# Routing tables by one-hot products instead of scatters, and a reordered end, in a strided-attention and mixture-of-experts kernel

## The chip, the cores and the metric

The kernel runs on one core of one Trainium2 chip. A core has TensorE (PE, matrix products into PSUM), VectorE (DVE), ScalarE (ACT), GpSimd (POOL) and SyncE (SP), each with its own instruction queue that runs in order; engines wait for each other through semaphores. The metric is the device time of one execution in microseconds (us). Profiles come from one execution that the hardware profiler recorded.

## The reference, cut to what matters

```python
# q, k, v: (8 batches, 8 heads, 576 positions, 64); the first 4 heads use mask_local, the others mask_strided
rel = pos[:, None] - pos[None, :]
mask_local = (rel >= 0) & (rel < 32)
mask_strided = (rel >= 0) & (pos[None, :] % 32 == pos[:, None] % 32)
attn = softmax(where(mask, q @ k.T / 8, -1e9)); x = attn @ v          # x: (8, 576, 512)

logits = x @ w_gate                                # 8 experts
local_gate = sigmoid(x @ w_local)
for b, s in order:                                 # a token keeps its predecessor's expert or takes its own
    fresh_e = argmax(logits[b, s])
    e = fresh_e if s == 0 or local_gate[b, s] < 0.5 else prev_e
    prev_e = e
    out[b, s] = softmax(logits[b, s])[e] * (relu(x[b, s] @ w1[e]) @ w2[e])   # w1: 512x1024, w2: 1024x512
```

## The kernel before, in words

There are three stages: attention (to 199 us of the profile), the experts, and a slow path (`general`) behind a branch on `flag`, which these inputs don't take.

`attention` walks over 32 pairs of heads (8 batches, 4 pairs each; two local, two strided) in steps `n`. Step `n` computes `scores` of pair `n` (L252; for strided pairs a mask product L246 first), the exponential on ACT, for local pairs a mask product on DVE (L263), the transposes `turn_x` of pair `n - 2` (L317), and `values` of pair `n - 1` (L276) with its normalisation `norm` (L289, L290). At a batch's end come `logits` (L336) and one step later `gates` (L354 and a chain of small DVE operations), which leave probabilities and a code for each token. `store_x` writes x to the DRAM tensor `xd` from SP's queue. A dictionary `also` puts further work at the end of given steps; weight sums of the first expert (L703) run from step 9, two a step. Constants (the masks among them) are made before the loop. All this is emitted under a manual schedule: the order in the code is the order in each queue.

The router works in two rounds of four batches. `Router.steps` finds each token's expert with scans over the codes and gives the token a slot: an index `idx` made of expert, place and tile. In both rounds a slot table `T` in DRAM is then filled by `scatters`, 20 indirect DMAs from POOL's queue (L577), each writing 8 bytes (token number, gate) for up to 128 tokens. `fetch` (L643) reads the table back to SBUF after round 1, `table` (L647) clamps its token numbers, and the experts gather rows of `xd` by it. Because round 0 alone fills a known part of expert 0's and 1's first tiles, `early` computes just those four columns of 128 slots in SBUF instead: a one-hot matrix `lane(i)` (128 tokens by 128 places, L620), a matrix `put` (token values times a one-hot of the column, L615), and 20 accumulated matmuls (L627), whose five outputs are put together to token number and gate (L632 to L637).

`Experts.run` goes through the experts, each with tiles of 128 tokens. Two tiles make a pair, computed with Strassen's seven products: `pair_hidden` (L807 with DVE additions L795 and ACT's relu L794, L814) and `pair_output` (L843; k operations L854 to L857; scatter of output rows L763). While a pair's output runs, the next pair's rows, gathered by L737, are scaled (L743), transposed (L750, copied out in L751) and summed (L759). `steps` is a list of places inside the pair at which other work is emitted: weight sums of the next expert (L703), and in the first two pairs round 1 of the router. After two pairs a `tc.Switch` on a number read into registers by `choose` picks one of seven arms, for up to three further tiles: a pair, a `single` (L898, L909) or a `half` (L919, L935). Before, the first two pairs of the run are expert 0's and 1's early tiles, then come expert 1's and 0's second pairs with their switches, then for each expert 2 to 7 its first pair, and its second pair with the switch. `flag` is loaded and tested after the last arm.

Of the kernel before, what the change touches and what calls it, by code (L numbers as in the profile page):

```python
# [18 lines left out]
P = 128  # L19
B, H, S, DH = 8, 8, 576, 64  # L20
D = H * DH
# [73 lines left out]
def attention_then_scomoe(ctx: ExitStack, tc: tile.TileContext, qkl, qks, vl, vs, wg, q, k, vl2, vs2, wg2, w1, w2, out):  # L95
# [7 lines left out]
    with ExitStack() as fast:  # L103
        once = fast.enter_context(tc.tile_pool(name="once", bufs=1))
        router = Router(once, dram, tc, ident)
        one = Weights(once)
        spot = (once.tile([P, 2, D], F32, name="x0"), once.tile([P, 2, DK, P], F32, name="xt"),
                once.tile([P, 4, 2, P], F32, name="tt"))
        with tc.manual_schedule():
            moe = Experts(nc, tc, xd, w1, w2, out, ident, router, one, spot)  # L110
            with ExitStack() as part:
                attention(part, tc, qkl, qks, vl, vs, wg, xd, ident, router, moe)
            with ExitStack() as part:
                moe.run(part)
        flag = router.flag


    redo = nc.values_load(flag, min_val=0, max_val=P + N,
                          skip_runtime_bounds_check_because="a count of at most 128 rows and of pairs")
    with tc.If(redo > 0):  # L120
# [22 lines left out]
def attention(ctx, tc, qkl, qks, vl, vs, wg, xd, ident, router, moe):  # L143
# [49 lines left out]
    for n, c in ((GK, GC), (GL, GR)):  # L193
# [20 lines left out]
        else:  # L214
            nc.vector.tensor_copy(maskS[:, 2 * GK:], cls)

    fold = consts.tile([P, E + 1], F32, name="fold")
    nc.vector.tensor_reduce(fold, ident.rearrange("p (k x) -> p x k", k=DK)[:, 0:E + 1], axis=AX.X, op=Alu.add)


    ci = consts.tile([P, E], I32, name="ci")
    nc.gpsimd.iota(ci, pattern=[[-1, E]], base=E, channel_multiplier=0)
    down = consts.tile([P, E], F32, name="down")
    nc.vector.tensor_copy(down, ci)
    pi = consts.tile([P, CH], I32, name="pi")
    nc.gpsimd.iota(pi, pattern=[[E * P, CH]], base=E, channel_multiplier=E)
    pos8 = consts.tile([P, CH], F32, name="pos8")
    nc.vector.tensor_copy(pos8, pi)
    start = consts.tile([P, CH], F32, name="start")
    nc.vector.tensor_scalar(start, pos8, float(E), None, Alu.is_equal)  # L230
# [165 lines left out]
    also = {n: [] for n in range(len(units) + 3)}  # L396
    also[2] = [router.constants]
# [6 lines left out]
    also[n] += [lambda: early.extend(router.early(bank, moe.spot)), lambda: early.pop(0)()]  # L404
    for n in range(m + 1, m + 6):
        also[n].append(lambda: early.pop(0)())
    for i, do in enumerate(router.scatters(0)):
        also[m + i // 2].append(do)
# [5 lines left out]
    for n in range(len(units) + 3):  # L414
# [20 lines left out]
        for do in steps[:2] if n >= 9 else []:  # L435
# [12 lines left out]
class Router:  # L448


    def __init__(self, pool, dram, tc, ident):
# [6 lines left out]
        self.tok = f("tok", [P, CH, B, 2], I32)  # L458
# [9 lines left out]
        self.io, self.jc = f("io", [P, P], BF16), f("jc", [P, 2, EARLY])  # L468
        self.vals = f("vals", [P, CH, RB, 5], BF16)
        self.put = f("put", [P, CH * RB, 5, 2 * EARLY], BF16)  # L470
        self.pool = pool
        self.T = dram.tile([P * NT, 2], I32, name="slots")

    def constants(self):
# [19 lines left out]
        ids = pool.tile([P, CH, B], I32, name="ids")  # L494
        nc.gpsimd.iota(ids, pattern=[[P, CH], [S, B]], base=0, channel_multiplier=1)
        nc.vector.tensor_copy(self.tok[:, :, :, 0], ids)
        for name, pattern, mult, o in (("io", [[1, P]], 0, self.io), ("jc", [[E, 2], [1, EARLY]], 0, self.jc),
# [5 lines left out]
        nc.gpsimd.iota(self.tab[:, :, 0], pattern=[[0, NT]], base=SKIP, channel_multiplier=0)  # L503
        nc.gpsimd.iota(self.tab[:, :, 1], pattern=[[0, NT]], base=0, channel_multiplier=0)
        nc.gpsimd.dma_start(out=self.rows(0, XT, E), in_=self.tab.rearrange("p (k e) v -> p k e v", e=E))

    def rows(self, k0, k1, e):

        return self.T.rearrange("(k p e) v -> p k e v", p=P, e=E)[:, k0:k1, 0:e]

    def steps(self, r, bank):
# [39 lines left out]
        def back():  # L551
# [16 lines left out]
            nc.vector.tensor_copy(self.tok.bitcast(F32)[:, :, bs, 1], p)  # L568
# [3 lines left out]
    def scatters(self, r):  # L572
        def one(t, b):
            m = min(P, S - t * P)

            def do():
                s = self.nc.gpsimd.indirect_dma_start(  # L577
                    out=self.T, out_offset=bass.IndirectOffsetOnAxis(ap=self.idx[0:m, t, b:b + 1], axis=0),
                    in_=self.tok[0:m, t, r * RB + b], in_offset=None, bounds_check=P * NT - 1, oob_is_err=False)
                self.tc.declare_no_dep(s.ins, group="slots", reason="scatters write different slots")  # L580
                self.tc.add_to_no_dep_group("slots", s.ins)
            return do
        return [one(t, b) for b in range(RB) for t in range(CH)]

    def early(self, bank, spot):
# [4 lines left out]
        lo, hi, code, lof = f("elo", [P, n], I32), f("ehi", [P, n], I32), f("ecode", [P, n]), f("elof", [P, n])  # L590
        at, rest, got = f("at", [P, n, 2 * EARLY], BF16), f("rest", [P, CH, RB]), f("got", [P, 5, 2 * EARLY])
        num, skip, gs = f("num", [P, 2 * EARLY]), f("skip", [P, 2 * EARLY]), f("gs", [P, 2 * EARLY])
        idx, val = flat(self.idx), self.vals.rearrange("p t b v -> p (t b) v")

        room = (spot[1].rearrange("p a k x -> p (a k x)").bitcast(BF16), spot[2].rearrange("p i a x -> p (i a x)").bitcast(BF16))
        lane = lambda i: room[2 * i // n][:, i % (n // 2) * P:(i % (n // 2) + 1) * P]

        def where():
# [6 lines left out]
            nc.vector.tensor_tensor(at, across(self.jc.rearrange("p k e -> p (k e)"), [P, n, 2 * EARLY]),  # L605
                                    spread(code, [P, n, 2 * EARLY]), op=Alu.is_equal)

        def what():
            v = [self.vals[:, :, :, i] for i in range(5)]
            nc.vector.tensor_copy(v[2], self.p)  # L610
# [3 lines left out]
            for i in range(5):  # L614
                nc.vector.tensor_tensor(self.put[:, :, i], at, spread(val[:, :, i], [P, n, 2 * EARLY]), op=Alu.mult)  # L615

        def lanes(a, b):
            def do():
                for i in range(a, b):
                    nc.vector.tensor_scalar(lane(i), self.io, lof[:, i:i + 1], None, Alu.is_equal)  # L620
            return do

        def products():
            o = bank()[:, 0:10 * EARLY].rearrange("p (v j) -> p v j", v=5)
            for i in range(n):
                m = min(P, S - i // RB * P)
                nc.tensor.matmul(o, lhsT=lane(i)[0:m], rhs=self.put[0:m, i], start=(i == 0), stop=(i == n - 1))  # L627
            nc.vector.tensor_copy(got, o)

        def numbers():  # L630
            tab = self.tab1.rearrange("p k e v -> p (k e) v")
            nc.vector.scalar_tensor_tensor(num, got[:, 0], 64.0, got[:, 1], Alu.mult, Alu.add)  # L632
            nc.vector.tensor_tensor(gs, got[:, 2], got[:, 3], op=Alu.add)
            nc.vector.tensor_scalar(skip, num, 0.0, SKIP + 64.0, Alu.is_equal, Alu.mult)
# [869 lines left out]
```

## Time and profile before

| | |
|---|---|
| median of 3 runs | 739.37 us (734.49 to 740.71) |
| profiled execution | 738.92 us |
| its span, first to last instruction | 737.2 us |
| mean granted TensorE clock | 0.959 |
| TensorE busy | 683.0 us (93%) |
| VectorE, ScalarE, GpSimd busy | 353.4, 195.5, 134.7 us |
| attention, experts | 0 to 199.6 us, 199.6 to 737.2 us |

A line of the groups names source line, engine, operation, output and input tiles and a count; after the bar stand busy us and the mean ns of one, then the idle time before them and what ended it. In the chain of work that ended last each line is a start, a length and what ran. A line in order of time has start, length, engine, line and operation; brackets at its end give the engine's idle time before it and what it waited for ("issue": nothing that the profile shows). PEld is TensorE's weight load, which overlaps its products.

### The profile page before, as it was taken

The page shows a single profiled execution, that of the slowest core. Times are in us where ns is not written, and L with a number is a line of the kernel's source. Part 1 is how long each engine was busy: PE and PEld are TensorE (multiplying, and loading weights), DVE is VectorE, ACT ScalarE, POOL GpSimd, SP SyncE. Part 2 cuts the span into 40 slices and gives each one's busy share as a digit, 9 for nine tenths or more (in the row PEclk, how much of TensorE's full clock was granted, in tenths as well). Part 3 has the DMA queues.
Part 4 walks back from the last instruction along what each step waited for, and adds up shares of the span by engine and source line. Part 5 has one row for each costly group of instructions (what it writes and reads, how often), then busy time and mean ns, then how long its engine had stood idle before and what let it go on. Part 6 is the DMA issues. An engine that isn't in the chain of part 4 may idle for free.

```text
span 737.2 us, 14832 instructions
## 1 busy us (share of the span) xinstructions
PE 683.0 (93%) x6034; PEld 586.5 (80%) x6034; DVE 353.4 (48%) x843; ACT 195.5 (27%) x357; POOL 134.7 (18%) x150
## 2 busy tenths in 40 slices
PE   7999999497899699999999999999999999999992
PEld 5878887385698589985998899999589899789961
DVE  6568766272466534451463265455126646524300
ACT  2544443141321122212222123122322222222210
POOL 3000001405127330221121120221012012111010
PEclk9999999597699899999999999999999999999997
DMA  9797887731360022615321711720171262010010
GB/s 325 275 328 267 279 286 256 249 84 52 95 228 30 3 86 67 238 38 173 109 74 47 254 47 50 251 73 21 39 257 59 76 210 66 32 37 30 18 50 13
DMA packets 37803, 95.33 MB, mean 129 GB/s; under 512 B 5230, under 2 KB 14446, under 8 KB 37632
## 3 DMA queue, kind: packets, MB, share of 16 engines
q1 hardware_dynamic: 29616, 73.77, 29.0%
q0 software_dynamic: 7488, 19.56, 8.4%
q8 instruction: 66, 1.08, 0.6%
q14 instruction: 105, 0.86, 0.4%
q10 hardware_dynamic: 528, 0.07, 0.1%
HBM read 74.41 MB, written 19.49 MB: 127 GB/s over the span
## 4 chain that ended last, share of the span: by engine, by line
PE 79%; issue 7%; DVE 5%; DMA 3%; another core or an unknown queue 3%; ACT 1%; POOL 1%; SPq 0%; DVEq 0%; POOLq 0%; ACTq 0%
PE mps L843 26%; PE lps L807 25%; PE vps L276 5%; PE sps L252 4%; PE tps L317 3%; PE lps L898 3%; PE mps L909 3%; PE xps L750 2%; DMA w1t<-in_w_dram 2%; PE mps L935 2%; PE lps L919 1%; PE sps L246 1%; PE tps L336 1%; PE vps L354 1%
## 5 line engine op out<-in xcount | busy, mean ns | idle before, releaser
L763 POOL DMA_INDIRECT out_dram<-y,tab x40 | 45.5, 1138 | 323.9 <-DVE y L795 217.4
L807 PE MATMUL lps<-tt,ws 128*128 128x128 f32 x768 | 91.5, 275 | 0.4 <-issue 0.2
L807 PEld LDWEIGHTS lps<-tt,ws 128*128 128x128 f32 x768 | 88.5, 192 | 0.8 <-DVE u L795 0.4
L843 PE MATMUL mps<-wt,k 128*128 128x256 f32 x384 | 85.6, 379 | 0.0
L843 PEld LDWEIGHTS mps<-wt,k 128*128 128x128 f32 x384 | 72.9, 190 | 9.9
L577 POOL DMA_INDIRECT slots<-tok,idx x40 | 40.9, 1023 | 147.5 <-DVE tok L568 135.9
L807 PE MATMUL lps<-xt,w1t 128*128 128x128 f32 x512 | 64.8, 281 | 2.6 <-ACT y L941 1.4
L807 PEld LDWEIGHTS lps<-xt,w1t 128*128 128x128 f32 x512 | 62.1, 196 | 6.1 <-ACT y L941 2.8
L795 DVE TENSOR_TENSOR h<-lps,u 128x512 f32<-128x512 f32 x48 | 33.2, 691 | 66.5 <-PE lps L807 57.3
L843 PE MATMUL mps<-w2t,h 128*128 128x256 f32 x256 | 61.3, 383 | 0.0
L737 POOL DMA_INDIRECT x<-xd,gi x40 | 40.4, 1009 | 112.5 <-PE lps L807 34.9
L252 PE MATMUL sps<-qk 64*128 64x96 f32 (+2 forms) x704 | 55.4, 288 | 4.9 <-issue 4.1
L252 PEld LDWEIGHTS sps<-qk 64*128 64x128 f32 (+2 forms) x704 | 45.5, 188 | 14.8 <-issue 12.5
L256 ACT ACTIVATE e<-sps 128x576 f32<-128x576 f32 (+1 forms) x64 | 41.2, 651 | 58.4 <-PE sps L252 40.8
L843 PEld LDWEIGHTS mps<-w2t,h 128*128 128x128 f32 x256 | 48.1, 193 | 6.0
L794 ACT ACTIVATE h<-h 128x512 f32<-128x512 f32 x48 | 30.3, 630 | 75.5 <-DVE h L795 71.7
L794 ACT ACTIVATE h<-lps 128x512 f32<-128x512 f32 x28 | 16.5, 594 | 86.8 <-PE lps L807 58.8
L795 DVE TENSOR_TENSOR u<-lps,p 128x512 f32<-128x512 f32 x16 | 11.1, 692 | 57.9 <-PE lps L807 32.3
L807 PE MATMUL lps<-xt,ws 128*128 128x128 f32 x256 | 33.1, 285 | 6.0 <-DVE h L795 6.0
L743 ACT ACTIVATE x<-x,tab 128x512 f32<-128x512 f32 (+1 forms) x40 | 27.2, 718 | 40.6 <-DMA x<-xd,gi 26.9
L807 PEld LDWEIGHTS lps<-xt,ws 128*128 128x128 f32 x256 | 31.5, 201 | 6.2 <-DVE h L795 6.2
L276 PE MATMUL vps<-vl,e 128*64 128x65 f32 x768 | 29.4, 235 | 7.0 <-issue 4.7
(222 smaller groups left out, 977.4 us busy)
## 6 DMA issues: line engine op xcount, KB each, us to landing
w1t<-in_w_dram SPq DMA_DIRECT2D x8, 2048.0 KB
w2t<-in_w_dram SPq DMA_DIRECT2D x8, 2048.0 KB
qk<-in_qkl_dram SPq DMA_DIRECT2D x16, 592.0 KB
qk<-in_qks_dram SPq DMA_DIRECT2D x16, 576.0 KB
vl<-in_vf_dram SPq DMA_DIRECT2D x8, 780.0 KB
vs<-in_vg_dram SPq DMA_DIRECT2D x8, 639.8 KB
xd<-xl SPq DMA_DIRECT2D x16, 288.0 KB
xd<-xs SPq DMA_DIRECT2D x64, 63.0 KB
```

Source lines behind the costliest of these rows:

```text
L252: nc.tensor.matmul(ps[0:m, h, c:c + w], lhsT=t[r, S + j * width:S + j * width + m], rhs=t[r, j * width:j * width + w], start=(u.local and ...
L256: nc.scalar.activation(e[0:kb, :, 0:n], ps[0:kb, :, 0:n], Act.Exp, bias=0.0, scale=1.0 / DH ** 0.5)
L276: nc.tensor.matmul(ps[a * HALF:(a + 1) * HALF, h, i], lhsT=u.e[0:m, h, q0:q0 + HALF], rhs=vt[0:m, j, 2 * i2 + h], start=(i == 0 and h == 0 ...
L317: nc.tensor.transpose(ps[:, t], src[:, t], ident)
L577: s = self.nc.gpsimd.indirect_dma_start(out=self.T, out_offset=bass.IndirectOffsetOnAxis(ap=self.idx[0:m, t, b:b + 1], axis=0), in_=self.t ...
L737: self.nc.gpsimd.indirect_dma_start(out=r.x[0:r.m, i], out_offset=None, in_=self.xd[0:r.rows], in_offset=bass.IndirectOffsetOnAxis(ap=r.gi ...
L743: self.nc.scalar.activation(r.x[0:r.m, i], r.x[0:r.m, i], Act.Copy, scale=r.gate[i][0:r.m])
L763: s = self.nc.gpsimd.indirect_dma_start(out=self.out, out_offset=bass.IndirectOffsetOnAxis(ap=r.si[i][0:r.m], axis=0), in_=y[0:r.m, i], in ...
L794: relu = lambda o, i: nc.scalar.activation(o, i, Act.Relu)
L795: add = lambda o, i, p: nc.vector.tensor_tensor(o, p, i, op=Alu.add)
L807: nc.tensor.matmul(ps[:, f], lhsT=m[:, kk, f * P:(f + 1) * P], rhs=v[:, kk], start=(start and f == 0 and kk == 0), stop=(kk == 1), skip_gr ...
L843: nc.tensor.matmul(ps[:, 0:256], lhsT=m[:, f], rhs=v[:, f], start=(start and f == 0), stop=(f == 3), skip_group_check=True)
```

## The change

1. The scatters, the DRAM table, its initial store, `fetch` and the old `table` go. A new `Router.table(r, ...)` builds all 56 columns of slots by one-hot products in both rounds. The second round adds onto the first's result. The column products (`put`) are now made on POOL, in 15 instructions a round; the lanes are made on DVE four at a time. Free tiles serve as room: the weight-sum tiles `t` of the weights at hand, `xt` or an output tile.
2. Masks: the second class mask (`classes(GL, GR)`) and other constants are made in steps 0 and 1 instead of before the loop.
3. The first expert's weight sums run from step 13, and the last eight of them (of w2) from step 29, after the table's products have read their room.
4. For experts 1, 0 and 7 the choice is loaded at the first place inside the pair rather than ahead of it.
5. The last expert runs its first pair with the switch and its second pair after the switch; `flag` is loaded inside that last pair, and the branch is told that the untaken side falls through.

```diff
-    redo = nc.values_load(flag, min_val=0, max_val=P + N, ...)
-    with tc.If(redo > 0):
+    with tc.If(redo > 0, preferred_fallthrough_block=False):
...
-    for n, c in ((GK, GC), (GL, GR)):
+    def classes(n, c):
...
+    classes(GK, GC)
...
+    also[0] = [lambda: classes(GL, GR)]
+    also[1] = [more_constants]
...
-    also[n] += [lambda: early.extend(router.early(bank, moe.spot)), lambda: early.pop(0)()]
+    lanes = moe.spot[1].rearrange("p a k x -> p (a k x)")
+    also[n] += [lambda: early.extend(router.table(0, bank, moe.W[0], lanes)), lambda: early.pop(0)()]
...
-    for i, do in enumerate(router.scatters(0)):
-        also[m + i // 2].append(do)
...
-        for do in steps[:2] if n >= 9 else []:
+        for do in steps[:2] if n >= (13 if len(steps) > 8 else m + 5) else []:
...
+    def table(self, r, bank, w, big):
...
         def where():
...
+            nc.vector.tensor_tensor(at, across(self.jc, [P, n, NT]), spread(code, [P, n, NT]), op=Alu.is_equal)
 
         def what():
...
+            for a in range(0, n, per):
+                m = min(n, a + per) - a
+                o = room[a // per][:, 0:m * wide].rearrange("p (i v j) -> p i v j", v=5, j=NT)
+                for i in range(5):
+                    nc.gpsimd.tensor_tensor(o[:, :, i], at[:, a:a + m], spread(val[:, a:a + m, i], [P, m, NT]), op=Alu.mult)
+
+        def some(a, b):
             def do():
+                for c in range(a, b, 4):
+                    l0, _, t = lanes[c >= nb]
+                    nc.vector.tensor_tensor(t[:, c - l0:c - l0 + 4], across(self.io, [P, 4, P]),
+                                            spread(lof[:, c:c + 4], [P, 4, P]), op=Alu.is_equal)
             return do
 
         def products():
+            o = bank()[:, 0:wide]
             for i in range(n):
                 m = min(P, S - i // RB * P)
+                nc.tensor.matmul(o, lhsT=lane(i)[0:m], rhs=put(i)[0:m], start=(i == 0), stop=(i == n - 1))
+            o = o.rearrange("p (v j) -> p v j", v=5)
+            if r:
+                nc.vector.tensor_tensor(got, o, got, op=Alu.add)
+            else:
+                nc.vector.tensor_copy(got, o)
...
+        return [where, what, some(0, n // 2 // 4 * 4), some(n // 2 // 4 * 4, n), products, numbers]
...
+            if index is None:
+                steps = [[lambda: chosen.append(choose(e))]] + steps
...
+        places[3] += [lambda: todo.extend(router.table(1, bank, W[1], other_y)), lambda: todo.pop(0)()]
+        for place in places[4:7]:
+            place.append(lambda: todo.pop(0)())
         output(self.first, W[0], pair_hidden(self.first, W[0], places), other, places)
         second = rows(0, 1, (2, 3))
-        places = slots(sums, [2, 2, 2, 2])
+        places = [[lambda: todo.pop(0)()]] + slots(sums, [3, 3, 2])
+        places[2] += [lambda: todo.pop(0)(), lambda: self.gather(second)]
...
-        places += [[lambda: next(arms), router.table, lambda: self.gather(second)]]
+        places += [[lambda: next(arms)]]
         h = pair_hidden(other, W[1], places)
-        router.fetch()
...
+        second = rows(0, e + 1, (2, 3))
+        rest(e + 1, W[e % 2], 1, nxt, [], second)
+        check = lambda: chosen.append(nc.values_load(router.flag, ...))
+        output(second, W[e % 2], pair_hidden(second, W[e % 2], [[check]]), None, [])
+        return chosen.pop()
```

## The prediction

> **What bounds the kernel now.** I read the page's totals and slices, then the chain that ended last, then stretches and the instructions in order of time where that chain leaves TensorE.
>
> ```profile
> PE 683.0 (93%) x6034; PEld 586.5 (80%) x6034; DVE 353.4 (48%) x843; ACT 195.5 (27%) x357; POOL 134.7 (18%) x150
> ...
> PEclk9999999597699899999999999999999999999997
> ...
> L577 POOL DMA_INDIRECT slots<-tok,idx x40 | 40.9, 1023 | 147.5 <-DVE tok L568 135.9
> ```
>
> TensorE (PE) is the bound, but the clock row dips in slices 7 to 13 (129 to 258 us): there PE isn't kept fed. The 40 scatters into the slot table all lie there. The chain says how much:
>
> ```profile
> 76.27 1.25 PE vps L354 x12
> 95.02 1.25 PE vps L354 x12
> 114.69 1.25 PE vps L354 x12
> 152.44 1.25 PE vps L354 x12
> 173.35 1.24 PE vps L354 x11
> 198.32 1.28 PE vps L354 x12
> ...
> 229.50 3.73 PE lps L807 x32
> ...
> 268.88 12.50 PE lps L807 x112
> ...
> 410.54 12.51 PE lps L807 x112
> ...
> 436.01 12.50 PE lps L807 x112
> ```
>
> L354 (gates) comes once a batch: 18.75 us apart undisturbed, then 37.75, 20.91 and 24.97. A pair of experts' tiles takes 436.01 - 410.54 = 25.47 us undisturbed, the second pair of the run 268.88 - 229.50 = 39.38. Inside the bad stretches (columns: stretch; us; busy and count of PE, PEld, DVE, ACT, POOL; clock; DMA share; GB/s):
>
> ```profile
> 176.00:181.00 5.00, 3.11 (x14) 2.21 (x15) 0.00 (x0) 0.00 (x0) 3.81 (x4) 0.50 0.03 4
> 240.00:245.00 5.00, 2.27 (x14) 1.56 (x12) 0.16 (x1) 0.60 (x1) 3.78 (x5) 1.00 0.02 1
> ```
>
> PE, DVE and ACT all stand while POOL issues scatters and the DMA engines are empty (3% and 2%). No data wait explains that: the releasers read "issue" or an unknown queue.
>
> [...] The trace agrees in kind: between 128 and 136 us it holds no instruction transfer at all, and the engines resume about when one lands. I read the stalls as fetches held up by the scatters' tiny writes; this is an inference. [...] The trace agrees only for POOL's side: a scatter issue of 0.97 us takes 1.41 when DVE runs such an operation.
>
> ```profile
> 218.69 0.69 DVE L855 TENSOR_TENSOR k<-k,h 128x512 f32<-128x512 f32 x1
> 218.83 1.41 POOL L577 DMA_INDIRECT slots<-tok,idx  x1 [0.30 <-issue]
> ...
> 222.34 0.91 POOL L577 DMA_INDIRECT slots<-tok,idx  x1 [0.30 <-issue]
> ```
>
> **The change part by part.** The sum is made against the profiled execution's 738.92 us (span 737.2 and 1.7 around it), 0.45 below the median of 739.37.
>
> *Scatters, table fetch and clamp go.* Batch 114.69 to 152.44: 37.75, less 18.75 and less 1.55 for the slot and back products that lie in it: 17.4 lost. Next batch: 20.91 less 19.4 (0.6 of old products in it): 1.5. The last batch has only the drain: by adding its PE pieces and the serial copies between them I estimate 14, so 24.97 - 14 = 11.0. Second pair: 39.38 - 25.47 = 13.9, which also holds the wait for table fetch and late gather (L737 at 260.75, its x scaled at 264 and 266). Sum 43.8. The 0.98 us table fetch and the initial table store leave POOL's queue without further gain.
>
> *Wide products come.* Per round 20 matmuls of 280 bf16 columns instead of 20 of 20 (0.60 us for all 20, round 0 only). [...] at L246's pitch, 252 columns in 0.18 us here, 4.0. I take 2.4: +4.2 in all, upper end +7.4. They are in PE's queue, so nothing hides them.
>
> *POOL builds the operands.* 15 multiplies a round, ten of 392 elements and five of 336: [...] PE waits for them in the products; every later PE instruction is queued behind that wait, and DVE's and ACT's work behind those. Round 0: the casts before them end near 132.5 on an unstalled clock; the products stand three steps on, near 145.4, so the cover is 12.9 us. Round 1: they start about 24 us after the first pair's start (16.8 to its output part, then DVE's six table operations 2.2, h and k operations 3.5, sums 1.3, casts 0.9, the first of them a little before that mark), and the products come at 33.4: cover 9.4. [...] in round 0 DVE has five 512-element comparisons (0.69 each, the price of such a DVE row) and six small operations of the gates in that window, [...] In round 1 fifteen such operations lie in it (six L703 sums of 0.68, five comparisons, four L759 of 0.42: 9.2): [...] I take the lock: 17.0, lower end 3.0.
>
> *DVE's own load.* The twenty 0.17 us comparisons and 0.84 of old products in round 0 become five of 0.69 and one 1120-element comparison of 1.3: much the same. In the second pair eight W[1] sums (5.5 us) now fall into three steps with numbers and arms, so k2 is 0.7 late; with a cooler clock after the waits I take +2.0 (0 to 4).
>
> *First masks first.* PE waits 2.29 us at 12.37 for e.
>
> ```profile
> 12.37 2.87 PE L276 MATMUL vps<-vl,e 128*64 128x65 f32 x48 [2.29 <-DVE e L263]
> ...
> 726.16 0.91 POOL L763 DMA_INDIRECT out_dram<-y,tab  x1 [8.59 <-ACT y L941]
> ```
>
> The moved work (twelve DVE operations of 0.20 to 0.29 and three on POOL, then seven more) doesn't vanish; norm of the first unit, at 14.24, moves only to about 14.3. So the next turn (17.42) gains about 1.3 of 2.3 (0 to 2.3).
>
> *Sums of W[0] moved.* The eight w1 sums from step 9 to 13 drop the 0.96 us wait for w1t; the eight w2 sums (0.68 each) go to steps 29 to 32, beside PE's drain. Taken as 0 (-1 to +1); if DVE is late there it shows in the last L354.
>
> *Choices inside a layer, second gather two places earlier.* Neither 268.88 nor 294 shows PE waiting at a choice, since matmuls queued before it keep PE busy: 0. Without that cover it is a gap as ACT's behind a switch at 537.69 (4.65 us), of which PE lost 0.35. The gather (two POOL issues of about 1 us) goes ahead of a scatter that nothing waits for: 0; its gain is in the 13.9.
>
> *Last pair behind the last switch, early flag.* Work is the same. After the last scatter's issue ends at 727.07 the span runs 10.1 us on. A row gather lands in about 2.05 us here (issued by 704.55, scaled at 706.62). Flag load and the taken branch leave the end; the landing stays, and an unconditional jump over the slow path too. I take -4.5, and -0.5 for one addition (0.42) in place of two copies (0.76): -5.0 (-2 to -7.5).
>
> Sum: -43.8 + 4.2 + 17.0 + 2.0 - 1.3 - 5.0 = -26.9, so 738.9 - 26.9 = 712.
>
> **The rivals.** *No lock.* POOL's reads go beside DVE's: waits 3.0 instead of 17.0, cooling and DVE 1.0 instead of 2.0: 738.9 - 41.9 = 697. For it: in this trace DVE was never held by POOL. Against: POOL here never reads wide operands beside DVE.
>
> *Multiplies dearer, or fetches still held.* At 1.3 us a multiply with the lock, about 12 us more wait; or gathers (40 stay) hold fetches as scatters did, and a quarter of the 43.8 stays: 11. Either gives about 724. For it: the stall at 171.4 began with two gathers. Against: pairs of gathers elsewhere show none.
>
> *POOL becomes the bound: slower.* Place: the wait at the two products. Without lock it is 30p - 22.3 us for a multiply of p us; all else gains 43.8 - 4.2 - 2.0 + 6.3 = 43.9, so it decides from p = 2.2. At p = 2.8: 738.9 - 43.9 + 61.7 = 757. For it: broadcast and bf16 operands on POOL aren't priced by any row. [...]
>
> **How the numbers follow.** Forecast 712: 0.52; no lock 697: 0.30; 724: 0.14; slower 757: 0.04. The range 694 to 723 takes in the first two with their bounds (products +3, tail and start about 3 either way) and leaves out half of the 724 case, the slower case and a little of the fastest. About 1% is what a measurement of this kernel can tell from no change (the three times shown spread over 0.8%). Faster by over 1% are the first three cases almost whole, 0.94; the fourth gives slower 0.04; 0.02 lies between.
>
> **What would show it.** Gates' L354 about 19 us apart from batch 4 to 6; PE's waits for POOL at the wide products, about 5 and 12 us; [...] second pair near 41 us (25.5, 12, 2.4 and 1); last scatter to end about 5.5 us. The prediction is wrong if stalls of all engines persist without scatters, if multiplies cost 2 us, or if POOL and DVE don't hold each other.

## The result and the profile after

In the first runs the median fell from 738.69 us (4 runs, 734.49 to 740.71) to 727.58 us (4 runs, 725.24 to 729.15). The ratio is 0.9864, with a 95% interval from 0.9824 to 0.9904: 11 us faster, where 27 were forecast. The profiled execution took 728.88 us (span 727.1). In the four groups of experiments below, each on a different chip, the kernel before takes 702 to 704 us (90 executions, 698 to 710). Run again beside it on one of these chips, the changed kernel is 20 us slower. That is the main finding.

The page of the changed kernel, with its totals, the clock row and the group of the new POOL multiplies:

```profile
PE 681.1 (94%) x6054; PEld 584.7 (80%) x6054; DVE 371.4 (51%) x842; ACT 195.2 (27%) x357; POOL 122.0 (17%) x135
...
PEclk9999999996999999999999999999999999999996
...
L606 POOL TENSOR_TENSOR wt<-wt,vals 128x392 bf16<-128x392 bf16 (+1 forms) x30 | 30.1, 1034 | 150.0 <-DVE wt L592 114.5
```

Between slices 7 and 13 one slice of the clock row is under 9 (slice 9, at 6), where the kernel before had four. The multiplies took 1.03 us on average. TensorE in order of time, from the gates of the fifth batch to the first pair:

```profile
113.67 1.25 PE L354 MATMUL vps<-fold,lT 128*128 128x9 f32 x12 [0.64 <-DVE sums L289]
...
135.86 1.25 PE L354 MATMUL vps<-fold,lT 128*128 128x9 f32 x12 [0.28 <-DVE sums L289]
...
144.58 0.41 PE L317 MATMUL tps<-ident,xs 128*128 128x128 f32 x2 [1.66 <-DVE sums L289]
...
146.98 2.08 PE L620 MATMUL tps<-wt,xt 128*128 128x280 bf16 x16
149.00 0.53 PE L620 MATMUL tps<-wt,wt 64*128 64x280 bf16 x3
...
161.02 1.25 PE L354 MATMUL vps<-fold,lT 128*128 128x9 f32 x12 [2.07 <-DVE sums L289]
...
178.58 2.19 PE L354 MATMUL vps<-fold,lT 128*128 128x9 f32 x12 [0.81 <-DVE lT L344]
180.70 1.65 PE L802 MATMUL lps<-xt,w1t 128*128 128x128 f32 x6
```

The gates are now 22.2, 25.2 and 17.6 us apart (37.8, 20.9, 25.0 before), and the first pair starts 18.8 us earlier. In round 0 PE waits for DVE, not for POOL itself. In the second pair the longest wait is for DVE too:

```profile
221.16 3.30 PE L802 MATMUL lps<-tt,ws 128*128 128x128 f32 x16 [4.19 <-DVE tt L754]
224.25 2.51 PE L620 MATMUL xps<-wt,y 128*128 128x280 bf16 x16
226.69 0.65 PE L620 MATMUL xps<-wt,wt 64*128 64x280 bf16 x4
...
241.90 3.51 PE L838 MATMUL mps<-w2t,h 128*128 128x256 f32 x8 [1.97 <-ACT q L854]
```

That POOL's multiplies hold DVE up (the prediction's "lock") is seen by laying two kernels side by side. First the changed kernel, in order of time, then the kernel with the multiplies on DVE (an experiment below), which has none on POOL:

```profile
204.37 16.45 POOL L606 TENSOR_TENSOR wt<-wt,vals 128x392 bf16<-128x392 bf16 x15 [33.31 <-issue]
...
206.43 2.23 DVE L698 TENSOR_TENSOR ws<-ws,w1t 128x512 f32<-128x512 f32 x2
...
208.58 2.59 DVE L612 TENSOR_TENSOR y<-io,elof 128x512 bf16<-128x512 bf16 x2
```

```profile
212.64 1.28 DVE L698 TENSOR_TENSOR ws<-ws,w1t 128x512 f32<-128x512 f32 x2
213.84 1.28 DVE L612 TENSOR_TENSOR y<-io,elof 128x512 bf16<-128x512 bf16 x2
```

The same two DVE operations take 2.2 to 2.6 us instead of 1.28 while POOL multiplies. Set against operations of the same form elsewhere in the changed kernel's trace, the 29 DVE operations that overlap POOL's multiplies in round 0 took 4.5 us longer in sum, and the 20 in round 1 took 7.4 us longer. The trace puts no wait of any engine down to a multiply itself: they cost PE time by way of DVE.

The last lines in order of time show the end of the work:

```profile
710.47 0.42 DVE L790 TENSOR_TENSOR y<-mps,v 128x256 f32<-128x256 f32 x1 [0.97 <-PE mps L838]
711.67 0.98 POOL L758 DMA_INDIRECT out_dram<-y,tab  x1 [0.90 <-POOLq L117]
```

The last scatter's issue ends at 712.65 and the span at 727.1: 14.4 us, against 10.1 before. The forecast was 5.5.

### The profile page after: what moved, and what is told of

It is laid out like the page before. It is cut to its first block, busy times and chain, and to the rows that moved or that the text cites. A ratio compares the mean times of both kernels' runs of the same rounds, so it can differ in the third digit from the quotient of the medians.

```text
span 727.1 us, 14808 instructions
## 1 busy us (share of the span) xinstructions
PE 681.1 (94%) x6054; PEld 584.7 (80%) x6054; DVE 371.4 (51%) x842; ACT 195.2 (27%) x357; POOL 122.0 (17%) x135
## 5 line engine op out<-in xcount | busy, mean ns | idle before, releaser
L802 PE MATMUL lps<-tt,ws 128*128 128x128 f32 x768 | 93.0, 278 | 5.4 <-DVE tt L754 4.2
L606 POOL TENSOR_TENSOR wt<-wt,vals 128x392 bf16<-128x392 bf16 (+1 forms) x30 | 30.1, 1034 | 150.0 <-DVE wt L592 114.5
L252 PE MATMUL sps<-qk 64*128 64x96 f32 (+2 forms) x704 | 51.7, 285 | 0.3 <-DMA qk<-in_qks_dram 0.2
L252 PEld LDWEIGHTS sps<-qk 64*128 64x128 f32 (+2 forms) x704 | 43.5, 187 | 8.5 <-issue 6.4
L838 PE MATMUL mps<-w2t,k 128*128 128x256 f32 x128 | 32.1, 396 | 2.1 <-DVE v L790 2.1
L746 ACT COPY xt<-xps 128x512 f32<-128x512 f32 (+1 forms) x38 | 19.9, 565 | 50.5 <-PE xps L745 50.4
L923 DVE COPY h<-lps 128x512 f32<-128x512 f32 x4 | 2.8, 691 | 56.4 <-PE lps L922 56.4
```

Of the source, the lines that this page charges most:

```text
L252: nc.tensor.matmul(ps[0:m, h, c:c + w], lhsT=t[r, S + j * width:S + j * width + m], rhs=t[r, j * width:j * width + w], start=(u.local and ...
L606: nc.gpsimd.tensor_tensor(o[:, :, i], at[:, a:a + m], spread(val[:, a:a + m, i], [P, m, NT]), op=Alu.mult)
L746: self.nc.scalar.copy(out=r.xt[:, i, :, 0:r.m], in_=ps[:, :, 0:r.m])
L802: nc.tensor.matmul(ps[:, f], lhsT=m[:, kk, f * P:(f + 1) * P], rhs=v[:, kk], start=(start and f == 0 and kk == 0), stop=(kk == 1), skip_gr ...
L838: nc.tensor.matmul(ps[:, 0:256], lhsT=m[:, f], rhs=v[:, f], start=(start and f == 0), stop=(f == 3), skip_group_check=True)
L923: nc.vector.tensor_copy(ht, ps)
```

## The experiments

The experiments ran in four groups. Each group was on a chip of its own, with the kernel before run beside it: 703.43, 702.43, 703.74 and 701.97 us. Whether one of the four is the chip of the first runs isn't recorded, so "the first runs" below means that chip at that time; "pair" means two tiles of an expert. Kernels are compared through the kernel before of their own group.

### The kernel before again

No edit.

> The kernel before, unedited, for its trace beside the other kernels of this group. Theory 1, the stalls of all engines are a matter of where it runs and not of its instructions: gates about 20.4, 19.3 and 13.8 us apart in the last three batches as in the kernel without scatters, first pair near 168.5, time 700 to 710. Theory 2, the scatters bring the stalls in some executions only: gaps of 38, 21 and 25, time 735 to 740.

Measured: 704.02 us, one execution. By stretch (columns: stretch; us; busy and count of PE, PEld, DVE, ACT, POOL; clock; DMA share; GB/s), the last three batches to the last gates, and the first and second pair:

```profile
116.49:138.20 21.71, 21.43 (x338) 17.87 (x339) 15.39 (x60) 9.26 (x17) 9.10 (x9) 0.92 0.81 273
138.20:157.96 19.76, 19.32 (x342) 16.06 (x343) 14.41 (x61) 9.26 (x17) 4.87 (x6) 1.00 0.56 176
157.96:171.78 13.82, 10.89 (x156) 8.30 (x156) 5.69 (x23) 6.66 (x14) 9.68 (x10) 1.00 0.45 121
172.99:202.82 29.83, 29.83 (x201) 27.68 (x198) 21.42 (x50) 7.04 (x14) 10.30 (x9) 0.94 0.43 150
202.82:235.31 32.49, 28.23 (x184) 25.05 (x182) 18.03 (x45) 6.21 (x11) 18.02 (x18) 0.95 0.14 43
```

POOL issues the same scatters in the same places, and the stalls of 37.75 and 24.97 are not there. Theory 1 holds: the same instructions run 35 us faster here. Next, the stretch in which the kernel before stood longest in the first runs, and then the matching one here (both start 13.3 us after the fifth batch's gates):

```profile
128.00:132.00 4.00, 1.93 (x16) 1.26 (x14) 0.00 (x0) 0.00 (x0) 3.09 (x4) 0.91 1.07 329
132.00:136.00 4.00, 0.58 (x2) 0.18 (x1) 0.77 (x3) 0.00 (x0) 3.09 (x4) 0.50 1.00 284
```

```profile
129.80:133.80 4.00, 4.00 (x79) 2.81 (x77) 3.20 (x9) 2.00 (x5) 3.09 (x4) 1.00 1.06 392
133.80:137.80 4.00, 4.00 (x76) 3.39 (x76) 2.52 (x13) 2.78 (x5) 3.09 (x4) 1.00 0.92 297
```

In both POOL issues four scatters in four microseconds and the DMA engines are full (92 to 107%); here PE never stands. So neither the scatters alone nor full DMA engines stop the engines. The empty DMA engines that I read before were those of two other stretches, and not of the longest stall. Over these eight microseconds the trace of the first runs holds no instruction transfer and this one holds three. Late instruction transfers thus go with the stall; whether they cause it or follow from it, the traces don't say.

### The changed kernel again

No edit.

> The changed kernel, unedited, beside the kernel before. Theory 1, the change costs what its own work costs (waits for DVE and POOL 12, products 5, late end 5, less 1 to 2 for the masks) and saves only what the scatters really cost, 3.5: 719 to 726 where the kernel before takes 703. Theory 2, the predicted saving is there too: below 700.

Measured: 722.41 us where the kernel before takes 702.43; ratio 1.0267 (1.0228 to 1.0305). The same stretches, and the third pair to PE's end:

```profile
110.89:133.12 22.23, 21.52 (x338) 17.85 (x339) 16.57 (x53) 9.14 (x17) 4.99 (x5) 0.92 0.80 287
133.12:156.38 23.26, 21.13 (x342) 17.19 (x343) 18.84 (x49) 9.18 (x17) 10.41 (x13) 1.00 0.51 151
156.38:170.21 13.83, 10.90 (x156) 8.32 (x157) 8.96 (x29) 6.58 (x14) 2.22 (x3) 1.00 0.48 141
171.42:204.06 32.64, 30.32 (x201) 27.61 (x198) 26.57 (x57) 6.93 (x14) 9.02 (x9) 0.95 0.37 135
204.06:243.26 39.20, 31.10 (x204) 27.72 (x203) 26.57 (x59) 6.01 (x11) 13.26 (x12) 0.91 0.08 28
243.26:702.37 459.11, 450.95 (x3017) 394.90 (x3015) 199.23 (x365) 104.76 (x190) 76.17 (x70) 1.00 0.28 95
```

The batch with the wide products (23.26) and both pairs are longer than in the kernel before, and so is the stretch to PE's end (455.60 there). Theory 1 holds: where the kernel before isn't stalled, the change costs 20 us.

### The kernel before without its scatters

```diff
-    for i, do in enumerate(router.scatters(0)):
-        also[m + i // 2].append(do)
...
-            place += [more.pop(0) for _ in range(n)]
+            pass
...
-            place += [more.pop(0) for _ in range(2)]
+            pass
```

> The kernel before without its 40 scatters into the slot table; it leaves out the filling of the table, so experts' tiles other than the first two pairs gather one row over and over and write nothing. Theory 1, the stalls of all engines come from the scatters: the stretches 114.69 to 152.44, 173.35 to 199.53 and the second pair lose 17, 8 to 11 and 10 to 14 us, and the time falls by 35 to 44 us to 695 to 704. Theory 2, the stalls come from the instruction fetch at these places whatever POOL issues: less than half of it goes, above 717.

Measured: 707.16 us, beside 703.43; ratio 1.0051 (1.0030 to 1.0072). The batches are 20.43, 19.34 and 13.82 us, and to 0.01 the same in the kernel of the next experiment, which has its scatters and ran on the same chip. The second pair:

```profile
198.35:227.81 29.46, 26.73 (x184) 23.93 (x182) 18.00 (x45) 6.21 (x11) 5.46 (x6) 1.00 0.15 47
```

29.46 against 32.97 in that kernel. So here the scatters cost 3.5 us, all in the second pair, and 4.0 more of this pair over 25.47 are not theirs. The expected times of both theories supposed stalls, and there were none to take away. What the scatters alone would give back where the first runs took place wasn't measured. New was the end: it takes 16.95 us instead of 9.35 (the kernel before run again), and eats the 3.5. The end is taken up below.

### The kernel before with the new end alone

```diff
-    with tc.If(redo > 0):
+    with tc.If(redo > 0, preferred_fallthrough_block=False):
...
-        for e in range(2, E):
+        for e in range(2, E - 1):
...
+        second = rows(0, e + 1, (2, 3))
+        rest(e + 1, W[e % 2], 1, nxt, choose(e + 1), [], second)
+        chosen = []
+        check = lambda: chosen.append(nc.values_load(router.flag, ...))
+        output(second, W[e % 2], pair_hidden(second, W[e % 2], [[check]]), None, [])
+        return chosen.pop()
```

> The kernel before with only the new end: the last expert's first pair ahead of the switch's arm, its second pair behind the switch, flag loaded inside that pair, the branch told that the untaken side falls through. As predicted: 5 us faster, 733 to 735. Theory 1, the new end is what cost the changed kernel its gain: 3 to 6 us slower, 742 to 745. Rival: within 1.5 us, since the 14.5 us at the end of the changed kernel belong to what its earlier part left behind.

Measured: 703.87 beside 703.43; ratio 0.9993 (0.9971 to 1.0016). The rival holds: the new end costs nothing here. It takes 9.0 us with scatters, and 13.9 to 14.4 in the changed kernel, which has none.

### The branch in its default form

```diff
-    with tc.If(redo > 0, preferred_fallthrough_block=False):
+    with tc.If(redo > 0):
```

> The changed kernel with the branch on flag built as before (its default form), the flag still loaded inside the last pair. Theory 1, the branch form costs the end: the changed kernel's 14.5 us from the last scatter to the end of the span fall to 6 to 10, and the time from about 727.6 to 719 to 723. Theory 2, the end is long because POOL's last drain has to wait for something else (it took 6.70 us against 1.95 in the kernel before): the end stays 13 to 15 us and the time within 1.5 us of 727.6.

Measured: 719.52 beside 703.43; ratio 1.0226 (1.0184 to 1.0268). The end takes 11.70 us. The expected times started from 727.6, which this chip doesn't show; by the ratios this form saves about 3 us (1.0226 beside the changed kernel's 1.0267), with intervals that overlap. Both theories hold in part. POOL's sequencer records, counted in us from the end of the last scatter's issue, tell why (start, then duration in brackets; "update" is its semaphore update for the row DMAs, "drain" its last long drain):

```
kernel                             indirect DMAs  update        drain         end
before (first runs)                120            6.66 (0.64)   7.33 (1.95)   10.13
changed (first runs)               80             2.33 (1.78)   6.88 (6.70)   14.43
changed, default branch            80             2.43 (1.78)   4.24 (6.61)   11.70
before without scatters            80             7.49 (1.82)   9.33 (6.77)   16.95
before, new end                    120            2.89 (0.63)   6.13 (2.04)    9.00
before, masks, new end             120            2.59 (0.63)   5.83 (2.04)    8.70
before, masks, new end, default    120            2.46 (0.64)   3.13 (1.95)    5.93
changed, gathers doubled           116            2.64 (2.50)   7.80 (9.63)   18.29
```

With the form of the change, POOL waits for the last rows, updates, and only then jumps over the slow path, with 2.5 to 2.8 us from the update's end to the drain. In the default form it jumps while the rows still land, and the drain follows the update at once. That is 2.2 to 2.8 us. The drain is another matter: it is 6.6 to 6.8 us in every kernel with 80 indirect DMAs, none of which has the scatters, whatever the form, and 2.0 in every kernel with the scatters. The last row is the next experiment's.

### Gathers doubled

```diff
-        for i in range(r.n):
+        for i in list(range(r.n)) * (2 if r.rows == N else 1):
             self.nc.gpsimd.indirect_dma_start(out=r.x[0:r.m, i], ...)
```

> The changed kernel with every row gather from the full table issued twice, 118 indirect DMAs instead of 80. Theory 1, POOL's last drain grows with the number of indirect DMAs since some count starts anew, which happened between the 102nd and the 111th in the kernel before: the drain falls from 6.7 to about 2 us, and the end from 14.4 to about 9.7. Theory 2, the drain is long for want of the scatters into the slot table or for the form of the end: it stays at 6.7. Either way the stages before lose 0 to 4 us by the later gathers.

Measured: 748.67 us beside 702.43; ratio 1.064 (1.0596 to 1.0683). The trace holds 116 indirect DMAs, not 118. The drain took 9.63 us: the half of theory 1 that it grows with the number of indirect DMAs holds (0.08 us for each of 80 and of 116), and so does the update (1.78 to 2.50). The half on a restart falls: more DMAs didn't bring one. In the kernel before, the update grows from 1.31 to 2.23 us and is 0.46 at the next switch, after which it is 0.63 and the drain 1.95. What restarts it in kernels with scatters stays open. The doubled gathers also cost far more than the 4 us that I allowed, about half of it (13.7 us) in expert 0's second pair and its arm; this doesn't touch the reading of the end.

### The multiplies on DVE

```diff
-                    nc.gpsimd.tensor_tensor(o[:, :, i], at[:, a:a + m], ...)
+                    nc.vector.tensor_tensor(o[:, :, i], at[:, a:a + m], ...)
```

> The changed kernel with its 30 column multiplies on DVE instead of POOL. Theory 1, POOL's slow multiplies and its lock with DVE make PE wait (12.5 us in the changed kernel's trace): the kernel before made 400-element products of this kind in 0.17 us on DVE, so 15 take 2.5 to 4 us a round on DVE, most of the wait goes, and the time falls by 7 to 11 us to 717 to 721. Theory 2, DVE's serial chain in these stretches is the limit whoever multiplies: what POOL gives up DVE takes on, and the time stays within 3 us of 727.6.

Measured: 727.16 beside 703.43; ratio 1.0342 (1.0299 to 1.0385). This is a miss for theory 1: it isn't faster, and by the ratio if anything slower than the changed kernel. Theory 2 has the time, and the reason below is near its own. The fifteen took 6.94 us a round; my price was wrong, since the row of 0.17 us had 80 elements and not 400. The fifteen of round 0, the batch in which they lie and the next, and the two pairs:

```profile
133.27 6.94 DVE L606 TENSOR_TENSOR wt<-wt,vals 128x392 bf16<-128x392 bf16 x15
```

```profile
113.75:141.18 27.43, 21.44 (x338) 17.90 (x339) 22.19 (x69) 9.25 (x17) 0.00 (x0) 0.92 0.74 249
141.18:166.32 25.14, 24.86 (x343) 20.49 (x343) 15.71 (x49) 9.15 (x17) 1.79 (x2) 0.82 0.27 75
...
181.59:220.00 38.41, 32.56 (x200) 29.43 (x199) 32.40 (x78) 7.02 (x14) 0.13 (x1) 0.88 0.32 114
220.00:251.24 31.24, 28.96 (x204) 25.88 (x202) 19.83 (x53) 6.01 (x11) 5.95 (x5) 1.00 0.10 35
```

On DVE they stand ahead of what PE waits for: a normalisation in round 0 (6.0 us) and an addition in the first pair (5.9 us). The last three batches take 66.40 us, where the changed kernel run again takes 59.32; 3.6 of the difference is PE's own busy time at a lower granted clock (0.82 in the second of these batches). The two pairs take 69.65 against 71.84. So DVE gains a little in round 1 and loses more in round 0.

### Six multiplies a round instead of fifteen

```diff
-                for i in range(5):
+                for i in range(2):
                     nc.gpsimd.tensor_tensor(o[:, :, i], at[:, a:a + m], ...)
...
+    also[3] = [lambda: [nc.gpsimd.memset(moe.W[0].t[i], 0.0) for i in (1, 2, 3)]]
...
+        for i in (1, 2, 3):
+            nc.gpsimd.memset(W[1].t[i], 0.0)
```

> The changed kernel with 6 column multiplies a round on POOL instead of 15; it leaves out the three parts of the gates, so the output is zero, while token numbers, comparisons and wide products stay (their room is set to zero early). Theory 1, PE waits because POOL is busy with the multiplies and holds DVE: the batch with the wide products falls from 23.3 to 21.2 to 21.8 us apart, the first two pairs from 71.8 to 63 to 67 us, the time by 6 to 10 us. Theory 2, DVE's own chain of comparisons, sums and small steps sets it: less than 3 us of that goes.

Measured: 714.05 beside 703.74; ratio 1.0135 (1.0084 to 1.0185). That is 10.3 over the kernel before, where the changed kernel is 20.0 over it. The batch with the products and the two pairs:

```profile
135.31:156.46 21.15, 20.87 (x343) 17.20 (x343) 15.64 (x49) 9.15 (x17) 1.78 (x2) 1.00 0.54 168
...
171.52:203.94 32.42, 30.28 (x199) 27.55 (x198) 26.36 (x58) 6.92 (x14) 6.06 (x6) 0.95 0.38 136
203.94:237.20 33.26, 29.24 (x203) 25.96 (x202) 22.49 (x58) 6.01 (x11) 6.08 (x5) 1.00 0.09 33
```

23.26 became 21.15 and the pairs 71.84 became 65.68. Theory 1 holds: nine multiplies fewer give back 2.1 us in round 0 and 6.2 in round 1, and PE's wait for `tt` in the second pair falls from 5.8 to 1.7 us. Counted as above, DVE's operations beside the multiplies lose 1.6 and 3.2 us instead of 4.5 and 7.4.

### Round 1 on DVE, spread over three places

The multiplies of round 1 become a function `chunks`, called once at each of the places of `what` and of both `some`; the branch has its default form.

```diff
+        if r:
+            return [where, lambda: (what(), chunks(0, per, nc.vector)), lambda: (both[0](), chunks(per, 2 * per, nc.vector)),
+                    lambda: (both[1](), chunks(2 * per, n, nc.vector)), products, numbers]
```

> The changed kernel with the branch in its default form, and the second round's multiplies on DVE, a chunk of five in each of three places (round 0 stays on POOL). Theory 1, what the second round costs is POOL's lock and its late start: the first two pairs fall from 71.8 to 65 to 68 us, the time from 720 to 713 to 716. Theory 2, DVE has no room in these pairs: they stay at 69 to 72, as with all of them on DVE at one place (69.7), the time at 717 to 720.

Measured: 720.08 beside 703.74; ratio 1.0216 (1.0164 to 1.0269).

```profile
175.48:209.49 34.01, 30.36 (x202) 27.63 (x198) 27.92 (x69) 6.92 (x14) 0.00 (x0) 0.95 0.36 129
209.49:250.34 40.85, 34.78 (x204) 29.96 (x203) 24.68 (x63) 6.01 (x11) 6.42 (x5) 0.83 0.08 27
```

The pairs take 74.86 in the profiled execution, but that was the slowest of the four (723.80), and in its second pair PE was busy for 34.78 us at a granted clock of 0.83, where the changed kernel run again had 31.10 at 0.91. By the medians this kernel and the one in the default form with its multiplies on POOL can't be told apart (1.0216 and 1.0226). So theory 1 falls, and theory 2 has the time: nothing measurable is gained by moving the second round's multiplies between these two engines. That DVE has no room in these pairs is argued and not shown.

### Expert 5's weight load later

In all kernels with the new tables expert 4's first pair is longer than in the kernel before: 27.0 us in the changed kernel, 29.5 when run again, and between these in the others, against 25.5. PE stands with no data to wait for while the DMA engines are full (99% from 438 to 442). First the changed kernel run again, then the same place in the kernel before run again:

```profile
435.80 2.02 PE L802 MATMUL lps<-xt,w1t 128*128 128x128 f32 x16 [0.56 <-issue]
439.84 3.38 PE L802 MATMUL lps<-tt,ws 128*128 128x128 f32 x19 [2.02 <-issue]
```

```profile
428.23 2.02 PE L807 MATMUL lps<-xt,w1t 128*128 128x128 f32 x16 [0.56 <-issue]
...
430.09 3.74 PE L807 MATMUL lps<-tt,ws 128*128 128x128 f32 x32
```

```diff
+            if e == 4:
+                steps = slots(W[0].sums(nc.vector), [0] * 5 + [1, 1, 1, 3] + [1] * 8 + [2])
+                steps[2].append(lambda: W[0].load(nc, w1, w2, 5))
+            else:
                 steps = slots(load(e + 1, W[e % 2]), [0] * 5 + [1, 1, 1, 3] + [1] * 8 + [2])
```

> The changed kernel with the weight load of expert 5 issued two places later, inside expert 4's first pair instead of ahead of it. Theory 1, in the changed kernel PE's next instructions come late because their fetch stands behind this load (expert 4's first pair takes 29.5 us instead of 25.5 in every kernel with the new tables): the pair takes 25.5 to 26.5 and the time falls by about 3 us. Theory 2, the pair is slow for another reason (its rows or its sums are late): it stays at 28 to 29.5.

Measured: 721.74 beside 701.97; ratio 1.0279 (1.0213 to 1.0345). The pair took 27.56, but the edit didn't do what it was for: SP's queue ran ahead, and the load was still issued 4.9 us before the pair, as in the unedited kernel. It tells nothing; that PE's instructions come late behind this load is argued and not shown. The kernel before speaks against the load as the whole cause: it too issues it 4.9 us before the pair, its DMA engines are as full (102% and 99% in the six microseconds from 428), and PE doesn't stand. The cause stays open.

### Masks and end, tables left as they were

The kernel before with the new masks and the new end of the earlier diff; scatters stay.

```diff
-    for n, c in ((GK, GC), (GL, GR)):
+    def classes(n, c):
...
+    classes(GK, GC)
...
+    def more_constants():
...
+    also[0] = [lambda: classes(GL, GR)]
+    also[1] = [more_constants]
```

> The kernel before with the first masks first and the new end alone; scatters stay. Theory 1, both parts help a little when the tables are left as they were: 1.5 us by the masks (gates of the first batch at 35.8 instead of 37.3) and 1 by the end, so 700 to 702 where the kernel before takes 703. Rival: what is gained at the start is lost by the next wait, within 1 us.

Measured: 699.69 beside 702.43; ratio 0.9966 (0.9946 to 0.9987). Theory 1 holds. The first gates stand at 34.92 instead of 37.54 us in the kernel before run again. Over all traces they stand at 37.3 to 37.5 with the old masks and at 34.9 to 36.8 with the new, so that single traces put the masks' gain anywhere between 0.5 and 2.6 us.

The same with the branch in its default form:

```diff
-    with tc.If(redo > 0, preferred_fallthrough_block=False):
+    with tc.If(redo > 0):
```

> The kernel before with the first masks first and the last pair behind the last switch with flag loaded inside it, the branch in its default form; scatters stay. Theory 1, in its default form the far jump runs beside the landing of the last rows, while the other form jumps after it: 2.2 to 2.7 us less than in the last group's kernel with the other form, the end at 6 to 7 us, the time 5 us under the kernel before (697 where that takes 702.5). Rival: the end is set by the last rows' landing and POOL's drain, so the form doesn't matter here: 699.5 to 700.5.

Measured: 698.18 beside 703.74; ratio 0.9907 (0.9868 to 0.9946). The end takes 5.93 us, and theory 1 holds. This version beats the kernel before, and by the ratios the changed one too. How it does where the first runs took place wasn't tried: no later run met such stalls.

## Why the prediction was wrong

The forecast of 712 was 16 us too low for the first runs, and its direction didn't hold when both kernels were run again. That the change was faster at all in the first runs rests on stalls that no later run had; the 3.0 to 3.5 us that the scatters cost elsewhere wouldn't have paid for the new work. By its steps:

**"Scatters, table fetch and clamp go", -43.8: the step that failed first.** It took the stalls of all engines for the scatters' own cost, which leaves with them. The sizes of the undisturbed stretches were right (20.43, 19.34 and 13.82 against my 20.3, 19.4 and 14). But elsewhere the same scatters in the same places stall nothing, so the stalls need more than the scatters, and what they need lay where or when the first runs took place. From the fifth batch's gates to the end of the second pair the kernel before took 154.0 us in the first runs and 117.6 elsewhere (the kernel with the new end alone), the changed one 140.2 and 132.4. Of 36.4 us of stalls 28.6 thus went with the change, and 7.8 stayed although the scatters were gone, in part as a lower granted clock (0.77 in the last batch, 1.00 when run again). To this come the 3.0 to 3.5 us that the scatters cost elsewhere. Besides, 4.0 of the second pair's 13.9 stay without any scatter. The step was worth about 32 and not 43.8. That the 28.6 went because the scatters went isn't shown, as no kernel without scatters alone ran there. Nor is it shown why both kernels stalled there, or whether instruction fetches were held; my inference stays an inference.

**Tail, -5.0: measured +4.3.** It falls into three parts by the table above. The new end by itself is worth nearly what I said: 10.13 (9.35 when run again) to 5.93, -3.4 to -4.2 against my -4.5, in the default form. The form that the change uses gives back 2.6 (what the other parts leave; 2.2 to 2.8 where the two forms were compared), since the jump then comes after the last wait; I knew of the jump and took it as the same in both. The drain (4.75) and the update (1.14) come from taking the 40 scatters out of POOL's queue, as the kernel before without them shows (6.77 and 1.82), a cost of the first step that shows 500 us later. 5.93 + 2.6 + 4.75 + 1.14 = 14.4. In the changed kernel's trace 2.7 us lie between POOL's branch and its next record.

**POOL's operands with the lock, 17.0, and DVE's load, 2.0: the lock is there and the sum somewhat too large, but the wait stands elsewhere.** The trace of before has no multiply on POOL, so how long one takes, and with it the 17.0, was not shown by any measurement. When run again, the multiplies that DVE hardly held took 0.84 to 0.87 us (392 elements) and about 0.75 (336), fourteen of the thirty 1.19 to 1.36, and the mean with the lock was 1.03 in the first runs. The lock shows on DVE's side too, as quoted above (2.23 and 2.59 us instead of 1.28). I had PE wait for POOL at the wide products, about 5 and 12 us. No such wait stands there: POOL's multiplies were done, and PE waited ahead of the products for DVE, which the lock had held up (when run again 1.7 us in round 0, 2.3 and 5.8 in the two pairs). When run again, round 0 costs 5.7 us (110.89 to 171.42, against 113.72 to 168.52 with scatters) where I had 6.8, and round 1 costs 12.55 (71.84 against 59.29 without scatters) where I had about 15.4. The "no lock" rival is out, and so is a multiply of 2.2 us. The wide products took 2.7 and 3.1 us in the first runs (the second at a granted clock of 0.86) instead of 2.4, which rested on no trace and was a little low. The cooler clock after waits, part of the 2.0, is in the trace of before: 0.59 from 250 to 255 us, where PE was busy throughout, after a stretch of five microseconds with 0.96 us of work.

**First masks, -1.3: right, measured -1.45 in the first runs.** The first gates moved from 37.28 to 35.83 us. The wait of 2.29 us went, and 0.87 of it came back through the first normalisation, where I had 1.0:

```profile
15.62 1.15 PE L317 MATMUL tps<-ident,xl 128*128 128x128 f32 x6 [0.87 <-DVE sums L289]
```

**W[0] sums and choices, 0: within their bounds**, 2.1 us of wait at the gates of the seventh batch apart, which was 0.3 when run again.

**Not in the prediction:** expert 4's first pair, 1.5 us in the first runs and 3.9 when run again.

Together, by stretch of the two profiled executions (738.92 and 728.88 us): up to the fifth batch's gates -1.0 where -1.3 was forecast, from there to the end of the second pair -13.9 where -20.6 was, from there to PE's end +0.3 where nothing was, and after PE's end +4.5 where -5.0 was. The 16.8 us that the forecast missed are 9.5 at the end, 6.7 in the middle and 0.5 elsewhere. The 6.7 are 11.7 that the first step was too large, less 5.0 that the two rounds cost less than forecast (18.25 instead of 23.2, when run again).

Nearest in number came the rival of 724, "multiplies dearer, or fetches still held", in its second half: a quarter of the 43.8 stays, 11 us. About 11.8 did, 7.8 of stalls and 4.0 that were never the scatters'. Its reason, that the gathers hold the fetches, isn't shown: elsewhere the same gathers run without stalls.

The rival on the other side named POOL as the bound. Where the change is slower it is so by the sum of smaller terms, none of them that one. When run again, with terms from the traces of several runs: -2.5 masks, +5.7 round 0, +12.55 round 1 less 3.0 for the scatters there (32.49 to 29.46), +3.5 from the third pair to PE's end, which expert 4's first pair (3.9) more than fills, and +4.55 end: 20.8, against 20.0 between the medians.

## What to carry to other kernels

A stall of all engines that no wait explains should be seen again on another chip before a change is priced against it; here it was worth 36 us in the first runs and nothing in four groups on four chips. Work moved to POOL beside a busy DVE can cost DVE's time too (4.5 and 7.4 us here), so price it by what DVE still has to do in that stretch, and look for the place before the engine. What follows the last instruction is part of the kernel: the form of the last branch and the indirect DMAs in POOL's queue moved the end between 5.9 and 18.3 us.

## What the hardware showed beyond that

In kernels without the scatters POOL's last drain and its semaphore updates lengthen with the indirect DMAs issued: the drain took 6.70 us after 80 and 9.63 after 116, the update at the end 1.78 and 2.50. In kernels with the 40 scatters the update drops from 2.23 to 0.46 us near the end and the drain is 2.0. The cause of that drop stays open.

DVE's bf16 multiplies of 392 or 336 elements with a broadcast operand took 0.46 us each (6.94 for fifteen), where POOL's took 0.75 to 0.87 undisturbed, and were still no gain, since they stood in DVE's queue.

A multiply on POOL and a DVE operation with two inputs lengthened each other: two DVE operations of 512 elements went from 1.28 to as much as 2.6 us, and the multiplies from about 0.84 (392 elements) or 0.75 (336) to 1.2 or more.
